# Seven-product second layer in the full chunks of batches 1 to 7 of a fused FFT filter and mixture-of-experts kernel, with the shrink subtractions on GpSimd

## The chip, the core and the metric

The kernel runs on one core of one Trainium2 chip. The time is device time in microseconds (us), median of several executions. Executions of one kernel agree within about 0.3% for the kernel before and within about 1% for the slowest variants here. Engines are named as in the profile: PE is TensorE (PEld its weight loads), DVE is VectorE, ACT is ScalarE, POOL is GpSimd, SP is the engine that issues most DMAs. The kernel's tiles lie in two on-chip memories: the results of matmuls in PSUM, all others in SBUF. An evacuation is a copy of a result out of PSUM.

## The reference, cut to what matters

```python
# x: (8, 2496, 256)
X  = rfft(x, axis=1)                                  # over the 2496 positions
Yr = Xr @ w_r - Xi @ w_i + b_r
Yi = Xr @ w_i + Xi @ w_r + b_i
Y  = sign(Y) * maximum(abs(Y) - 0.01, 0)              # "shrink", on Yr and Yi
x  = irfft(Y, axis=1)
# one expert per batch, chosen from the mean over positions
h      = maximum(x[b] @ w1[e], 0)                     # (2496, 1024)   first layer
out[b] = gate * (h @ w2[e])                           # (2496, 256)    second layer
```

## The kernel before

Each batch passes through a forward transform, a complex product, the shrink, an inverse transform, and then the two expert layers. The batches are pipelined: while batch b is in its expert layers, batch b+1 is in its transforms. A list scheduler inside the program fixes the order of instructions on every engine when the kernel is built, from a planned duration for each operation. On the chip, each engine works through its own list in order: the seven kernels below that share one plan (the changed one, e3 to e7, e9) show the same order of instructions on PE, DVE and ACT, at different times.

**The shrink**, for each of 5 groups of frequency bins in a batch (batches 2 to 7). `z` is the product, `cl` is `z` clamped to plus and minus 0.01, and `Y = z - cl`. Four subtractions move data between the two halves of the partitions:

```python
oc_ = S.op("DVE", 0.34, cl_, vt(f + 0.03), deps=z_ops, lat=0.48)
def y_(_, cell=cell):
    Y = cell["Y"]
    for r in range(2):
        for i in range(2):
            s = slice(64 * i, 64 * i + 64)
            nc.vector.tensor_sub(out=Y[64*r : 64*r+64, :, i],
                                 in0=cell["z"][s, r], in1=cell["cl"][s, r])
oy = S.op("DVE", 1.5, y_, vt(f + 0.03), deps=[oc_], lat=1.62)   # planned: 1.5 us, result after 1.62
```

The inverse transform's matmuls (line L547 in the profile) read `Y`.

**The second layer**, for a chunk of 512 tokens, is by default 32 matmuls of 256 columns (L1438): 4 token tiles times 8 slices of the hidden dimension. In the chunks listed in `FAST` it is done as seven block products in place of eight (Winograd's form of Strassen's product): the chunk's tokens, the hidden dimension and the output columns are each cut in two. That takes 56 matmuls of 128 columns (L1252), four sums of the hidden values on DVE, and combinations of the products on the way out of PSUM:

```python
FAST = {(B - 1, c) for c in range(4)}            # last batch only
# add_fast, per chunk: four DVE sums of 128x1024 fp16, both inputs in SBUF
o1 = S1 = h[0,1] + h[1,1]      # L1219
o2 = S2 = S1 - h[0,0]          # L1222
o3 = S3 = h[0,0] - h[0,1]      # L1226 (in place)
o4 = S4 = h[1,0] - S2          # L1229
# ... seven products; three DVE adds (L1276) and four scaled copies on ACT or DVE (L1267, L1270)
# once per batch, four DVE sums of 128x512 of the second layer's weights: L1193 to L1196
```

## Time and profile before

| | before |
|---|---|
| median of 4 runs | 431.42 us |
| PE busy, of the profiled span | 417.4 us, 97% |
| DVE / ACT / POOL busy | 305.3 / 336.1 / 60.6 us |
| one batch in the repeating middle | 50.0 us |

This is one group of the profile's list; the columns after the bar are busy us, mean ns of one, and the engine's idle time just before these instructions, with what ended it.

```profile
L928 DVE TENSOR_TENSOR tt<-ps,bias 128x512 f16<-128x512 f32 x60 | 38.6, 686 | 18.1 <-PE ps L914 17.9
```

DVE is idle because it waits for PE's results, not the reverse. And this is the same fact for a stretch of exactly two batches (length, then busy us of PE, PEld, DVE, ACT, POOL, each with its count of instructions; then granted PE clock, DMA share, GB/s):

```profile
210.60:310.59 99.99, 99.99 (x839) 75.91 (x838) 78.52 (x163) 78.20 (x154) 15.19 (x26) 1.00 0.86 207
```

PE does not pause at all in these 100 us.

### The profile page before, as it was taken

How to read it: one execution, taken by the hardware profiler on the slowest of the kernel's cores; microseconds unless marked ns; L12 is line 12 of the kernel's file. 1: busy time of each engine (PE TensorE's matmuls, PEld its weight loads, DVE VectorE, ACT ScalarE, POOL GpSimd, SP SyncE). 2: the span in 40 equal slices, each digit the busy share in tenths (PEclk: the TensorE clock that was granted, in tenths of full speed). 3: DMA queues.
4: the chain of work that ended last, by engine and by line, in shares of the span. 5: the costliest groups of instructions: out<-in, count | busy, mean ns of one | idle time of the engine just before them, and what ended most of it. 6: DMA issues, size and time to landing. Idle time of an engine off the chain costs nothing.

```text
span 429.5 us, 9604 instructions
## 1 busy us (share of the span) xinstructions
PE 417.4 (97%) x3601; PEld 315.9 (74%) x3601; DVE 305.3 (71%) x635; ACT 336.1 (78%) x654; POOL 60.6 (14%) x104
## 2 busy tenths in 40 slices
PE   5988999999999999999999999999999999999996
PEld 2557777887777877778677876778777787777775
DVE  1697865777777797787967787677977878414561
ACT  3789888787967887779866798678877788778884
POOL 5553100001003020033000320031200030001000
PEclk9999999999999999999999999999999999999999
DMA  7999797929885996889885998959978276521222
GB/s 151 234 172 163 129 279 238 216 75 181 230 270 106 232 186 195 251 171 203 191 247 194 197 203 209 283 117 218 194 220 253 86 166 126 181 91 56 65 99 92
DMA packets 71847, 76.98 MB, mean 179 GB/s; under 512 B 7128, under 2 KB 45744, under 8 KB 71800
## 3 DMA queue, kind: packets, MB, share of 16 engines
q1 hardware_dynamic: 58834, 56.23, 44.7%
q0 software_dynamic: 12704, 19.88, 29.1%
q8 instruction: 28, 0.46, 0.4%
q10 hardware_dynamic: 262, 0.25, 0.2%
q14 instruction: 19, 0.16, 0.1%
HBM read 57.54 MB, written 37.49 MB: 221 GB/s over the span
## 4 chain that ended last, share of the span: by engine, by line
PE 92%; DVE 3%; DMA 2%; ACT 2%; POOL 1%; issue 1%; SPq 0%; DVEq 0%; POOLq 0%
PE ps L1389 31%; PE ps L1438 27%; PE ps L914 9%; PE ps L718 4%; PE ps L547 4%; PE ps L812 3%; PE ps L1058 3%; PE ps L1252 3%; PE ps L876 3%; PE ps L1323 2%; DMA xin<-in_x_dram 1%; PE ps L751 1%; PE ps L754 1%; DMA ysb<-in_w_i_dram 1%; DVE z L766 1%; ACT ysb L1074 1%
## 5 line engine op out<-in xcount | busy, mean ns | idle before, releaser
L1402 ACT ACTIVATE hs<-ps 128x512 f16<-128x512 f32 (+3 forms) x313 | 172.1, 568 | 65.3 <-PE ps L1389 61.3
L1389 PE MATMUL ps<-ysb,w1s 128*128 128x512 f16 (+3 forms) x688 | 182.6, 359 | 0.1
L1438 PE MATMUL ps<-w2s,hs 128*128 128x256 f16 x1056 | 150.9, 272 | 0.0
L1438 PEld LDWEIGHTS <-hs 128*128 128x128 f16 x1056 | 102.0, 98 | 38.3 <-issue 0.9
L1389 PEld LDWEIGHTS <-w1s 128*128 128x128 f16 x688 | 73.9, 113 | 17.9 <-issue 0.7
L956 DVE TENSOR_TENSOR Y<-z,cl 64x512 f16<-64x512 f16 x120 | 50.4, 420 | 2.7
L928 DVE TENSOR_TENSOR tt<-ps,bias 128x512 f16<-128x512 f32 x60 | 38.6, 686 | 18.1 <-PE ps L914 17.9
L914 PE MATMUL ps<-w,XT 128*128 128x256 f16 x360 | 49.9, 273 | 0.1
L914 PEld LDWEIGHTS <-XT 128*128 128x128 f16 x360 | 34.9, 98 | 9.9 <-DVE XT L895 0.6
L1455 ACT ACTIVATE ost<-ps,gbc 128x512 f32<-128x512 f32 (+1 forms) x57 | 38.4, 675 | 2.7 <-PE ps L1438 1.9
L937 DVE TENSOR_TENSOR z<-ps,tt 128x512 f16<-128x512 f32 x60 | 38.7, 683 | 0.2
L1074 DVE CAST ysb<-ps 128x468 f16<-128x468 f32 (+1 forms) x37 | 21.4, 587 | 22.7 <-PE ps L1058 20.0
L554 ACT CAST V<-ps 128x512 f16<-128x512 f32 x52 | 30.2, 598 | 0.6
L822 ACT CAST A<-ps 120x512 f16<-120x512 f32 x46 | 26.0, 613 | 3.1 <-PE ps L812 3.1
L884 ACT CAST XT<-ps 128x512 f16<-128x512 f32 x41 | 24.3, 596 | 0.0
L1074 ACT CAST ysb<-ps 128x468 f16<-128x468 f32 (+1 forms) x47 | 21.8, 533 | 2.4 <-PE ps L1058 2.4
L1150 POOL DMA_DIRECT2D w1s<-in_moe_w_dram x8 | 6.0, 755 | 122.3 <-PE ps L1058 111.6
L547 PE MATMUL ps<-Y,ti 128*128 128x256 f16 x140 | 23.0, 272 | 0.0
L884 DVE CAST XT<-ps 128x512 f16<-128x512 f32 x19 | 13.1, 689 | 13.8 <-PE ps L876 13.0
L812 PE MATMUL ps<-xin,wa 117*120 117x512 f16 x66 | 22.8, 380 | 0.1
L1404 DVE TENSOR_SCALAR hs<-ps 128x512 f16<-128x512 f32 (+3 forms) x31 | 17.4, 568 | 7.3 <-PE ps L1389 6.5
L1058 PE MATMUL ps<-wi,V 120*128 120x117 f16 (+1 forms) x308 | 22.5, 213 | 0.0
(112 smaller groups left out, 476.5 us busy)
## 6 DMA issues: line engine op xcount, KB each, us to landing
out_dram<-ost SPq DMA_DIRECT2D x71, 256.0 KB
scr<-V SPq DMA_DIRECT2D x35, 256.0 KB
xin<-in_x_dram POOLq DMA_DIRECT2D x21, 390.0 KB, 9.8
XB<-fwd SPq DMA_DIRECT2D x30, 256.0 KB
V<-scr SPq DMA_DIRECT2D x14, 504.0 KB
fwd<-A SPq DMA_DIRECT2D x18, 360.0 KB
w1s<-in_moe_w_dram POOLq DMA_DIRECT2D x8, 512.0 KB, 7.1
w2s<-in_moe_w_dram POOLq DMA_DIRECT2D x8, 512.0 KB, 8.1
```

The lines of the kernel that those rows point to most:

```text
L547: nc.tensor.matmul(pv[:, D * i : D * i + D], ti[:, 4 * q + k, :], cell["Y"](k))
L812: nc.tensor.matmul(pa[0:120, :], wa, xin_t[b][:, xcol(2 * gp) : xcol(2 * gp) + 2 * D])
L884: COPY[eng](out=cell["X"][:, ch, :, 0:2].rearrange("p a r i k -> p a i r k"), in_=hc["p"].rearrange("p (a i r k) -> p a i r k", a=2, i=2, ...
L914: nc.tensor.matmul(pm[:, D * a : D * a + D], cell["X"][:, ch, a, t].rearrange("p i k -> p (i k)"), w4[:, ch, t, :], start=(ch == 0), stop= ...
L928: nc.vector.tensor_add(out=cell["tt"][:, r], in0=cell["T", 2].rearrange("p (a c) -> p a c", a=2), in1=bias[:, r].unsqueeze(1).to_broadcast ...
L937: nc.vector.tensor_add(out=cell["z"][:, r], in0=cell["T", 1 - r].rearrange("p (a c) -> p a c", a=2), in1=cell["tt"][:, r])
L956: nc.vector.tensor_sub(out=Y[64 * r : 64 * r + 64, :, i], in0=cell["z"][s, r], in1=cell["cl"][s, r])
L1074: COPY[eng](out=yv[:, :, 12 * gb : 12 * gb + 3 * nf].rearrange("p a (g j) -> p a g j", j=3), in_=pi[:, 0 : 117 * nf].rearrange("p (g a j) ...
L1389: nc.tensor.matmul(ph[:, 0:nl], w1v[:, ch, fc // 4, :, fc % 4], ysb_t[b][:, ch, ns : ns + nl], start=(ch == 0), stop=(ch == 1))
L1402: nc.scalar.activation(out=o, in_=i, func=AFT.Relu)
L1438: nc.tensor.matmul(oc["p"][:, i, :], cell["hs"][:, ft, ts], w2s_t[b][:, ft, :], start=(ft == 0), stop=(ft == E - 1))
L1455: nc.scalar.activation(out=ost[:, 0:n], in_=oc["p"][:, 0:n], func=AFT.Copy, scale=gbc_t[b])
```

## The change

The intent is to save PE columns: the seven-product form is to serve all full chunks of batches 1 to 7. DVE gets much work by that, so the shrink subtractions go to GpSimd, which is nearly idle. The token tiles of the seven-product form take alternate tokens, so that a partition holds two neighbouring rows of the output and stores them as one run.

```diff
-    FAST = {(B - 1, c) for c in range(4)}
+    FAST = {(b, c) for b in range(1, B) for c in range(4)}
@@ shrink
-                        nc.vector.tensor_sub(
+                        nc.gpsimd.tensor_sub(
                             out=Y[64 * r : 64 * r + 64, :, i],
                             in0=cell["z"][s, r], in1=cell["cl"][s, r])
-            oy = S.op("DVE", 1.5, y_, vt(f + 0.03), deps=[oc_], lat=1.62)
+            oy = S.op("POOL", 4.9, y_, vt(f + 0.03), deps=[oc_], lat=5.1)
@@ add_fast: token tiles (one of the seven operands shown)
-        A = {"11": lambda f, t: cell["hs"][:, f, m * t : m * t + m],
+        A = {"11": lambda f, t: cell["hs"][:, f, t:th:2],
...
-                        "(i p) c -> p i c", p=m),
+                        "(p i) c -> p i c", i=2),
```

The scheduler is thus told that the four GpSimd subtractions take 4.9 us, with the result after 5.1.

More of the change, by code (lines that the diff above doesn't have):

```diff
@@ L1234, in add_fast @@
         o4 = s_op("s4", 0, s4, vt(0.3), [o2])
-        A = {"11": lambda f, t: cell["hs"][:, f, m * t : m * t + m],
-             "12": lambda f, t: cell["hs"][:, 4 + f, m * t : m * t + m],
-             "22": lambda f, t: cell["hs"][:, 4 + f, th + m * t : th + m * t + m],
-             "S3": lambda f, t: cell["hs"][:, f, th + m * t : th + m * t + m],
-             "S1": lambda f, t: fc["S"][:, 0, f, m * t : m * t + m],
-             "S2": lambda f, t: fc["S"][:, 1, f, m * t : m * t + m],
-             "S4": lambda f, t: fc["S"][:, 2, f, m * t : m * t + m]}
+        A = {"11": lambda f, t: cell["hs"][:, f, t:th:2],
+             "12": lambda f, t: cell["hs"][:, 4 + f, t:th:2],
+             "22": lambda f, t: cell["hs"][:, 4 + f, th + t : nl : 2],
+             "S3": lambda f, t: cell["hs"][:, f, th + t : nl : 2],
+             "S1": lambda f, t: fc["S"][:, 0, f, t:th:2],
+             "S2": lambda f, t: fc["S"][:, 1, f, t:th:2],
+             "S4": lambda f, t: fc["S"][:, 2, f, t:th:2]}
         w2 = lambda k, h: lambda f: w2s_t[b][:, 4 * k + f, P * h : P * h + P]
```

## The prediction

> **What bounds the kernel now.** I read the page's engine row first, then the table of equal windows over the repeating middle, then the groups of instructions, then the chain that ended last.
>
> ```profile
> PE 417.4 (97%) x3601; PEld 315.9 (74%) x3601; DVE 305.3 (71%) x635; ACT 336.1 (78%) x654; POOL 60.6 (14%) x104
> ...
> 200.00:250.00 50.00, 50.00 (x421) 37.85 (x419) 39.26 (x81) 39.02 (x77) 7.59 (x13) 1.00 0.85 204
> 250.00:300.00 50.00, 50.00 (x423) 38.05 (x421) 39.26 (x81) 39.19 (x77) 7.61 (x13) 1.00 0.87 206
> ...
> PE 92%; DVE 3%; DMA 2%; ACT 2%; POOL 1%; issue 1%; SPq 0%; DVEq 0%; POOLq 0%
> ```
>
> The window rows give length, then busy time of PE, PEld, DVE, ACT and POOL. One batch takes about 50 us (its first L812 matmuls stand in the chain at 210.60, 260.68 and 310.59), and in such a window PE is busy all of it at full clock, DVE 39.3, ACT 39.2, POOL 7.6. Busy PE need not be PE at its peak, so I checked the pace: in the chain 8 matmuls of 256 columns take 0.87 us, 8 of 128 columns 0.45, 24 of them 1.34. That is 109 and 56 ns each, within a few ns of columns over 2.4 GHz. So **TensorE's column stream is the bound**; DVE and ACT have 10.7 us of idle time each per batch.
>
> **What the Trainium skill says.** (1) "TensorE: Matmul & The Clock Gate", Back-to-back issue gap: an isolated gap is N/2.4 + 2.5 ns, but a sustained stream with weight loads is given as about 81 ns at N=128. The trace disagrees with the 81: 56 ns with a load each. I use 56. (2) "SBUF — State Buffer", Who interferes with whom: a DVE instruction with two SBUF inputs, or in a two-port mode, shares a port with a GpSimd instruction that reads SBUF, and the second to issue blocks until the first has finished. The kernel before has one spot that agrees:
>
> ```profile
> 19.91 1.50 POOL L420 TENSOR_SCALAR V<-tf 128x512 f16<-128x512 f16 x1
> 21.37 0.78 POOL L422 COPY V<-tf 128x512 f16<-128x512 f16 x1
> ...
> 20.84 0.16 DVE L1122 TENSOR_SCALAR lsb<-ps 128x8 f32<-128x8 f32 x1
> 20.96 0.73 DVE L779 TENSOR_SCALAR cl<-z 128x1024 f16<-128x1024 f16 x1
> 21.73 0.97 DVE L781 TENSOR_TENSOR Y<-z,cl 128x1024 f16<-128x1024 f16 x1
> ```
>
> The columns are start and duration. The DVE clamp, normally 0.43 us, takes 0.73 when it starts 0.45 before the end of a GpSimd instruction; the subtraction of two SBUF tiles, normally 0.69, takes 0.97 when it starts 0.42 before the end of the next. Each loses what remained of the GpSimd instruction, less some 0.15 us[...]. DVE instructions that read PSUM keep their 0.68 there. (3) "GPSIMD Engine Reference", Performance versus the Vector engine: about 2.6 cycles per element for two inputs. At its 1.2 GHz, 512 elements make 1.11 us plus dispatch; I estimate 1.2 us for one 64x512 subtraction. The trace before has none.
>
> **The change part by part.** The durations that I use:
>
> ```profile
> L956 DVE TENSOR_TENSOR Y<-z,cl 64x512 f16<-64x512 f16 x120 | 50.4, 420 | 2.7
> L1276 DVE SCALAR_TENSOR_TENSOR ost<-ps,gbc,ost 128x256 f32<-128x256 f32 x12 | 5.8, 482 | 10.5 <-ACT ost L1267 7.7 <-PE ps L1252 2.8
> L1226 DVE TENSOR_TENSOR hs<-hs 128x1024 f16<-128x1024 f16 x4 | 2.7, 684 | 0.0
> ```
>
> *TensorE.* 24 more chunks (4 in each of batches 1 to 6) take the seven-product form. Each drops 32 matmuls of 256 columns and adds 56 of 128: 32 x 109 = 3.48 us out, 56 x 56 = 3.11 in, so -0.36 us a chunk, -1.45 a batch, **-8.7 us in all**. That is 2.0% and the most the change can give, at a period of 48.5 us.
>
> *Alternate-token tiles.* Weight loads now step by two elements. L1438 already does that and takes 98 ns a load, as the contiguous loads of L1252 do; only the step of four of L1389 takes 113. Nothing lost on PE. Output rows stay in runs of two tokens, so the stores keep their shape. Worth zero by itself.
>
> *DVE.* I took the changed instruction counts from the compiled order and the durations from the groups above. Over the kernel: +96 sums of 128x1024 at 0.687 = +65.9; +24 weight sums at 0.42 = +10.1; +76 combining instructions at 0.482 = +36.6; -120 subtractions = -50.4; evacuations moved to ACT and back by the kernel's own scheduler, net -15. Sum +47 us over 6 batches, or +7.8 of summed duration; neighbours overlap by some 5%, so I take **39.3 + 7.3 = 46.6 us busy per batch**. That is already 96% of the 48.5 that PE would need.
>
> *ACT.* +92 evacuations of 128x256 at 0.483 = +44.4, -47 output evacuations = -32, +22 ysb casts = +12.4, rest nearly even: +25 us, about 43.5 per batch. Busy, but not the bound.
>
> *GpSimd.* 20 subtractions per batch, 20 x 1.2 = 24 us on top of 7.6: 32 us of 50. Not the bound, but its chain clamp, subtract, inverse matmul grows from 1.7 to about 5 us for each of 5 groups, which the static order allows for.
>
> *Port.* Here lies the decision. DVE instructions of a batch that use two SBUF inputs or the two-port mode: 16 sums, 4 weight sums, 5 XT sums, 5 clamps, 30 in all. Each clamp releases four GpSimd subtractions, 4.8 us in a row, and the compiled DVE order often puts sums right behind a clamp. I walked one batch by hand, letting DVE run back to back and the two engines take turns. Behind clamp 1 stand four weight sums: three wait for a whole subtraction, about 1.1 us each, 3.4 in all. Clamp 2: two isolated sums, 0.45 + 0.95 = 1.4. Clamp 3: one, 1.05. Clamp 4: three, 3.1. Clamp 5: three, 2.95. **Sum 11.9 us a batch if the port is locked as the two events above suggest.** Then DVE needs 46.6 + 11.9 = 58.5 us, a period 8.5 over today's, and six periods make +51: about 482 us. If the port is only shared, or the waits partly fall into DVE's idle time, I put 4 to 6 us a batch: a period of 51 to 53, so 438 to 450.
>
> **The rivals.**
> 1. *TensorE stays the bound.* The port costs little, 46.6 us of DVE hides under 48.5, and the time is 431.6 - 8.7 = 423 plus a few us of stalls: 424 to 430. For it: DVE idles waiting for PE today (17.9 us before L928, 20.0 before L1074), and that slack can be eaten first. Against: 96% on an in-order engine leaves PSUM banks waiting, and the two collisions above were not free.
> 2. *DVE becomes the bound through the port*: 438 to 482, as worked out. For it: the two stretched instructions, and 24 us of reads placed in front of DVE's sums. Against: only two events, both against one-input GpSimd instructions.
> 3. *The longer subtraction chain stalls TensorE.* If four subtractions take 7 us instead of the 5 that the order was made for, the inverse matmuls (L547) wait up to 2 us five times a batch, up to +10 us a batch at worst, mostly the same time as in 2. Deferred x and weight loads behind subtractions in the GpSimd queue belong here too. The x loads have a slack of many us: the queue stood 31 us before the copy that heads them.
> 4. *Transfers.* Bytes do not change; DMA share of 0.85 stays. I give this nothing.
>
> **Range and chances.** Faster by over 2% needs 423.1 or less, which is the whole of the 8.7 us with no stall anywhere: 4%. Within 2% (up to 440) needs a period under 51.4, port waits plus stalls under some 4.8 us a batch: 26%. Slower: 70%. I weigh rival 1 by a fifth to a quarter, sharing or partial hiding by a quarter, the full lock by half, but trim the hand walk, since DVE falling behind spreads the collisions out: about 6 us a batch over the PE floor. 423 + 6 x 5 = **453 us**, range 427 to 482.
>
> **What would show each step.** PE: 1568 matmuls in L1252 at a pace of 56 ns where eight run together, and 288 left in L1438; if the pace is slower, the stride costs and the first step is wrong. DVE: windows of one batch with DVE busy near its whole length and PE well below it; if DVE shows 46 to 47 and PE all, rival 1 holds. Port: the mean of the sums (L1219, L1222, L1226, L1229) above 0.9 us instead of 0.687, L1193 to L1196 far above 0.42, while L928 and L937, which read PSUM, keep 0.68; if all keep their durations, the lock was wrong. GpSimd: L956 near 1.2 us when undisturbed. Chain: L547 idling for the GpSimd Y would show rival 3; the chain that ended last should move from 92% PE to a mix with DVE and POOL.
> The prediction is wrong most likely if GpSimd's subtraction is much shorter than 1.2 us or does not hold the port.

## The result and the profile after

The changed kernel takes **474.54 us** (4 runs, 472.51 to 476.92) against 431.42: 1.10 times as long, interval 1.094 to 1.106. Ratios here are the mean of one kernel's fast runs over that of the other's of the same rounds, so not quite the ratio of the medians. The predicted 453 us was too low by 21.5, in the right direction and inside the range (427 to 482).

The page of the changed kernel, its engine row, its chain that ended last, and the group of the moved subtractions:

```profile
PE 425.8 (90%) x4177; PEld 320.6 (67%) x4177; DVE 382.8 (81%) x686; ACT 353.8 (74%) x723; POOL 215.5 (45%) x224
...
PE 63%; DVE 24%; issue 6%; POOL 3%; ACT 1%; DMA 1%; DVEq 0%; ACTq 0%; POOLq 0%
...
L956 POOL TENSOR_TENSOR Y<-z,cl 64x512 f16<-64x512 f16 x120 | 153.9, 1282 | 160.6 <-DVE cl L946 97.5
```

PE fell from 97% to 90% of the span, and its share of the chain from 92% to 63%. DVE came into the chain. Two batches of the repeating middle, in the columns of the window row above:

```profile
221.91:338.29 116.38, 102.88 (x1032) 77.91 (x1030) 103.89 (x177) 85.18 (x178) 67.44 (x66) 0.97 0.74 176
```

The window runs, as the one before the change, from one batch's first L812 matmuls in the chain to those of two batches later. A batch takes 116.38 / 2 = **58.2 us** where it took 50.0. DVE is busy 51.9 us of it. Which waits does PE now have? This is the list of waits of PE in the changed kernel (who waited for whom; total us, times, longest):

```profile
PE ps L1058 <- DVE ysb L1074: 12.9, 5, 2.6
PE ps L914 <- DVE XT L895: 11.8, 13, 1.8
PE ps L1389 <- DVE hs L1404: 4.1, 2, 2.1
...
PE ps L1252 <- DVE ost L1270: 3.1, 2, 1.6
PE ps L812 <- DVE A L822: 2.5, 1, 2.5
PE ps L1252 <- DVE S L1222: 1.8, 6, 0.8
...
PE ps L547 <- POOL Y L956: 0.4, 2, 0.2
```

The six DVE lines add to 36.2 us, near the 37 us by which PE's idle time grew (475.2 - 425.8 = 49.4 against 429.5 - 417.4 = 12.1). PE waits for DVE, in many places, and hardly ever for the GpSimd result itself (0.4 us). Now DVE. Groups by shape, sums first, then an instruction that reads PSUM:

```profile
L1226 DVE TENSOR_TENSOR hs<-hs 128x1024 f16<-128x1024 f16 x28 | 29.6, 1058 | 0.0
L1222 DVE TENSOR_TENSOR S<-S,hs 128x1024 f16<-128x1024 f16 x28 | 29.6, 1057 | 0.6
L1219 DVE TENSOR_TENSOR S<-hs 128x1024 f16<-128x1024 f16 x28 | 25.3, 905 | 0.1
L1195 DVE TENSOR_TENSOR T<-w2s 128x512 f16<-128x512 f16 x7 | 7.7, 1100 | 0.0
...
L928 DVE TENSOR_TENSOR tt<-ps,bias 128x512 f16<-128x512 f32 x60 | 39.0, 680 | 1.8 <-PE ps L914 1.7
```

The sums that took 0.68 us in batch 7 of the kernel before now take about 1.0 on average, three of the four weight sums 1.0 to 1.1 for 0.42 (the first, L1193, kept its 0.42), while the addition from PSUM kept its 0.68. The clamp, with one input, kept its 0.42 as a rule, but took 1.38 in 2 of 30 cases. One spot shows why. The time line of DVE, then that of POOL, over the same microseconds (start, duration):

```profile
302.98 0.68 DVE L1219 TENSOR_TENSOR S<-hs 128x1024 f16<-128x1024 f16 x1
303.70 1.53 DVE L1222 TENSOR_TENSOR S<-S,hs 128x1024 f16<-128x1024 f16 x1
305.15 1.64 DVE L1226 TENSOR_TENSOR hs<-hs 128x1024 f16<-128x1024 f16 x1
306.71 0.68 DVE L1229 TENSOR_TENSOR S<-hs,S 128x1024 f16<-128x1024 f16 x1
```

```profile
301.81 1.16 POOL L956 TENSOR_TENSOR Y<-z,cl 64x512 f16<-64x512 f16 x1
303.02 1.66 POOL L956 TENSOR_TENSOR Y<-z,cl 64x512 f16<-64x512 f16 x1
304.75 1.48 POOL L956 TENSOR_TENSOR Y<-z,cl 64x512 f16<-64x512 f16 x1
```

The two engines take turns. A sum starts at 302.98; the GpSimd subtraction of 303.02 then needs 1.66 in place of 1.15: it waited about half a microsecond for that sum, and ended at 304.68. The next sum, issued at 303.70, ends at 305.23, which is 0.55 after that subtraction ended. The last subtraction ends at 306.23, and the sum issued at 305.15 ends at 306.79. With the series over, the fourth sum takes 0.68 again.

The trace also ties these sums to PE's waits. Between 110 and 410 us PE waited 20 times for over 0.8 us, and at each of them DVE was at a sum stretched to 1.2 us or more, or had been less than 1.5 us earlier. The five waits at L1058, up to 2.6 us and 12.9 in all, stand behind stretched weight sums (L1194 to L1196).

### The profile page after: what moved, and what is told of

Its sections match the earlier page's. It is cut to its first block, busy times and chain, and to the rows that moved or that the text cites. A ratio compares the mean times of both kernels' runs of the same rounds, so it can differ in the third digit from the quotient of the medians.

```text
span 475.2 us, 11058 instructions
## 1 busy us (share of the span) xinstructions
PE 425.8 (90%) x4177; PEld 320.6 (67%) x4177; DVE 382.8 (81%) x686; ACT 353.8 (74%) x723; POOL 215.5 (45%) x224
## 4 chain that ended last, share of the span: by engine, by line
PE 63%; DVE 24%; issue 6%; POOL 3%; ACT 1%; DMA 1%; DVEq 0%; ACTq 0%; POOLq 0%
PE ps L1389 21%; PE ps L1252 13%; PE ps L914 7%; PE ps L1438 5%; PE ps L718 3%; DVE S L1222 3%; PE ps L812 2%; PE ps L1323 2%; DVE S L1219 2%; PE ps L547 2%; POOL Y L956 2%; PE ps L876 2%; DVE S L1229 2%; DVE z L937 2%; PE ps L1058 2%
## 5 line engine op out<-in xcount | busy, mean ns | idle before, releaser
L956 POOL TENSOR_TENSOR Y<-z,cl 64x512 f16<-64x512 f16 x120 | 153.9, 1282 | 160.6 <-DVE cl L946 97.5
L1267 ACT ACTIVATE ost<-ps,gbc 128x256 f32<-128x256 f32 x108 | 51.9, 481 | 24.0 <-PE ps L1252 23.4
L1276 DVE SCALAR_TENSOR_TENSOR ost<-ps,gbc,ost 128x256 f32<-128x256 f32 x84 | 40.2, 479 | 30.7 <-ACT ost L1267 18.2
L1252 PEld LDWEIGHTS <-S 128*128 128x128 f16 x672 | 43.6, 98 | 15.9 <-DVE S L1222 4.4
L1074 ACT CAST ysb<-ps 128x468 f16<-128x468 f32 x68 | 32.8, 545 | 18.4 <-PE ps L1058 18.4
L1438 PE MATMUL ps<-w2s,hs 128*128 128x256 f16 x288 | 40.8, 272 | 0.0
L1252 PE MATMUL ps<-T,hs 128*128 128x128 f16 x448 | 35.2, 223 | 3.2 <-DVE ost L1270 3.1
L1252 PE MATMUL ps<-T,S 128*128 128x128 f16 x448 | 34.1, 219 | 2.2 <-DVE S L1222 1.8
L1404 DVE TENSOR_SCALAR hs<-ps 128x512 f16<-128x512 f32 (+3 forms) x44 | 26.6, 609 | 10.2 <-PE ps L1389 9.7
L1058 PE MATMUL ps<-wi,V 120*128 120x117 f16 (+1 forms) x308 | 23.0, 216 | 13.0 <-DVE ysb L1074 12.9
L1252 PE MATMUL ps<-w2s,hs 128*128 128x128 f16 x448 | 34.0, 219 | 0.0
L1058 PEld LDWEIGHTS <-V 120*128 120x128 f16 x308 | 19.9, 99 | 15.3 <-issue 13.6
```

The lines of the kernel that those rows point to most:

```text
L956: nc.gpsimd.tensor_sub(out=Y[64 * r : 64 * r + 64, :, i], in0=cell["z"][s, r], in1=cell["cl"][s, r])
L1058: nc.tensor.matmul(pi[:, 117 * i : 117 * i + M], V2[:, g, ch * P : ch * P + P], w)
L1074: COPY[eng](out=yv[:, :, 12 * gb : 12 * gb + 3 * nf].rearrange("p a (g j) -> p a g j", j=3), in_=pi[:, 0 : 117 * nf].rearrange("p (g a j) ...
L1252: nc.tensor.matmul(fc[dst[0]][0:m, dst[1], t, :], A[a](f, t), bb(f), start=start and t == 0 and f == 0, stop=f == 3, skip_group_check=True)
L1267: nc.scalar.activation(out=ost(t, h), in_=src, func=AFT.Copy, scale=gbc_t[b][0:m])
L1276: nc.vector.scalar_tensor_tensor(out=ost(t, h), in0=fc["F"][0:m, half], scalar=gbc_t[b][0:m], in1=ost(t, h), op0=ALU.mult, op1=ALU.add)
```

## The experiments

Theories. **Port:** GpSimd subtractions and DVE instructions with two SBUF inputs block each other; the sums stretch, DVE falls behind, and PE waits for DVE. **Load:** DVE has too much work, collisions or not. **Chain:** the path clamp, subtraction, inverse matmul became too long for the fixed order, and PE waits for GpSimd. **Tiles:** the alternate tokens cost PE or DMA something. Twelve kernels were run, in three lots; times of the kernel before in the same lots were 431.64, 431.68 and 431.12 us. e5 and e6 were executed twice, the others four to six times.

| run | differs from | time, us | ratio to before (95%) |
|---|---|---|---|
| e1_no_gpsimd | after: subtractions on DVE | 438.17 | 1.016 (1.014 to 1.017) |
| e2_gpsimd_only | before: subtractions on GpSimd | 432.72 | 1.004 (1.001 to 1.006) |
| e3_write_only | after: GpSimd writes 8 constants | 426.94 | 0.990 (0.988 to 0.992) |
| e4_contig_tiles | after: contiguous tiles | 475.84 | 1.103 (1.101 to 1.105) |
| e5_write_only_long | after: GpSimd writes 12 constants | 474.10 | 1.098 (1.094 to 1.103) |
| e6_read_copy | after: GpSimd copies, one input | 464.28 | 1.075 (1.073 to 1.078) |
| e7_split_subs | after: subtractions halved | 458.59 | 1.062 (1.060 to 1.064) |
| e8_two_chunks | e1: two of four chunks | 434.13 | 1.005 (1.004 to 1.007) |
| e9_write_only_ten | after: GpSimd writes 10 constants | 442.69 | 1.027 (1.026 to 1.029) |
| e10_longer_in_order | after: scheduler told 6.6 us | 478.27 | 1.110 (1.106 to 1.113) |
| e11_half_dose | after: two of four chunks | 444.26 | 1.030 (1.028 to 1.032) |
| e12_write_only_in_order | e10: GpSimd writes 12 constants | 447.37 | 1.037 (1.035 to 1.038) |

### The parts of the change, one at a time

**e1: subtractions back on DVE.**

```diff
-                        nc.gpsimd.tensor_sub(
+                        nc.vector.tensor_sub(
-            oy = S.op("POOL", 4.9, y_, vt(f + 0.03), deps=[oc_], lat=5.1)
+            oy = S.op("DVE", 1.5, y_, vt(f + 0.03), deps=[oc_], lat=1.62)
```

> The changed kernel with the shrink subtractions back on DVE; seven-product form and alternate-token tiles stay. Port theory (GpSimd subtractions and DVE sums block each other): the four kinds of sums go back to 0.68 us each, but DVE gets 8.4 us a batch of subtractions back, 46.6 + 8.4 = 55 us busy per batch, so DVE stays the bound: 458 to 470 us. Load theory (DVE simply has too much work, the port adds nothing): this must be slower than the changed kernel, over 480. Chain theory (the long wait for the GpSimd result stalls TensorE, DVE has room): back to 424 to 432.

Measured 438.17, a miss for all: much better than the port theory's number, against the load theory, and not quite the chain theory's. A hundred microseconds of its middle, and one kind of sum:

```profile
210.00:310.00 100.00, 98.11 (x1018) 74.78 (x1016) 96.12 (x207) 83.80 (x181) 15.14 (x26) 1.00 0.83 201
```

```profile
L1226 DVE TENSOR_TENSOR hs<-hs 128x1024 f16<-128x1024 f16 x28 | 19.1, 683 | 0.0
```

The sums are back at 0.68. DVE is busy 96% of the time, and yet PE gets 98%. My 55 us of DVE per batch was too much for two reasons: the kernel's scheduler hands more evacuations to ACT (740 ACT instructions for the changed kernel's 723), and neighbouring DVE instructions overlap by more than I had allowed. What follows: DVE carrying all the work, subtractions included, is 36 us faster than DVE relieved of them. The load theory falls.

**e2: the GpSimd subtractions alone, in the kernel before.** The same two lines of diff as in e1, the other way, applied to the kernel before.

> The kernel before with only the shrink subtractions moved to GpSimd. Port theory: DVE falls to about 31 us a batch, only the 5 clamps and 5 XT sums of a batch can collide and few do; TensorE stays the bound: 430 to 437. Load theory: the same, 430 to 433. Chain theory: five stalls of 1 to 2 us a batch, 455 to 470.

Measured 432.72, as port and load said. GpSimd was nearly as busy as in the changed kernel (199.9 us for 215.5), but there are few DVE instructions with two SBUF inputs to collide with. Those that there are do stretch: the XT sums (L895) took 0.607 us on average for 0.42, and the four weight sums of batch 7 took 1.26 to 1.38. DVE had room for it.

So each half alone costs little, 6.5 us and 1.1 us, and both together 43. The other 35 us exist only where DVE's sums and GpSimd's subtractions are in the kernel at once.

**e4: contiguous tiles in the changed kernel.**

```diff
-        A = {"11": lambda f, t: cell["hs"][:, f, t:th:2],
+        A = {"11": lambda f, t: cell["hs"][:, f, m * t : m * t + m],   # and so for all seven
-                        "(p i) c -> p i c", i=2),
+                        "(i p) c -> p i c", p=m),
```

> The changed kernel with the contiguous token tiles of the kernel before in the seven-product form (output rows stored one token at a time). All theories that put the cost on DVE and GpSimd: 470 to 478, as the changed kernel. If the weight loads with a step of two cost TensorE time: faster by 1% or more; if one-token rows load the DMA queues: slower by 1% or more.

Measured 475.84, the changed kernel's time within its scatter. The tiles are not where the time went, in either direction.

### Is it the reading of SBUF?

**e3: GpSimd as busy, but only writing.** One subtraction of two columns makes GpSimd wait for the clamp; then eight constant writes into `Y`. Its output is wrong, which doesn't matter for the time. The scheduled order is that of the changed kernel.

```diff
                 Y = cell["Y"]
+                nc.gpsimd.tensor_sub(out=Y[:, 0, 0, 0:2], in0=cell["z"][:, 0, 0, 0:2],
+                                     in1=cell["cl"][:, 0, 0, 0:2])
                 for r in range(2):
                     for i in range(2):
-                        s = slice(64 * i, 64 * i + 64)
-                        nc.gpsimd.tensor_sub(out=Y[64*r : 64*r+64, :, i],
-                                             in0=cell["z"][s, r], in1=cell["cl"][s, r])
+                        for _h in range(2):
+                            nc.gpsimd.memset(Y[64*r : 64*r+64, :, i], 0.01)
```

> The changed kernel, where GpSimd reads two elements of z and cl in one small subtraction and then writes a constant into Y eight times, about as long as the four subtractions, but reading no SBUF (wrong result on purpose). Port theory with blocking by GpSimd reads only: sums back to 0.68 us, 46.6 us of DVE a batch fits, 425 to 437 us. Load theory and chain theory: sums keep what they have or the waits stay, 465 to 480.

Measured **426.94 us**, 1.0% below the kernel before. The lines of this file are shifted by two, so L1228 is the in-place sum, L1226 in the others:

```profile
L1228 DVE TENSOR_TENSOR hs<-hs 128x1024 f16<-128x1024 f16 x28 | 19.1, 683 | 0.0
```

With the same DVE list and the same PE list, and GpSimd nearly as busy (193.1 us), the sums are undisturbed and the change would be a small gain. But one point was not clean: eight writes with their small subtraction last 4.6 us (median), while the four real subtractions last 4.8 to 5.9 in the changed kernel (median 5.3). A chain that is shorter than real might hide a chain effect. So I made it longer.

**e5: twelve writes**, `range(3)` in place of `range(2)` above.

> As the write-only stand-in, with twelve constant writes instead of eight: 12 x 0.52 + 0.3 = 6.6 us from the clamp to the end of Y, longer than the four real subtractions under collision (5.1 to 5.6 us). Port theory: GpSimd still reads nothing, the sums stay at 0.68 us, 425 to 434 us. Chain theory (the length of the GpSimd step stalls TensorE): at or above the changed kernel, 465 to 490.

Measured 474.10 us: the changed kernel's own time, against my expectation. Had I looked at the time alone, the port theory would have fallen here. The same sum, and the longest wait of PE:

```profile
L1228 DVE TENSOR_TENSOR hs<-hs 128x1024 f16<-128x1024 f16 x28 | 19.1, 684 | 0.0
```

```profile
PE ps L547 <- POOL Y L959: 39.6, 36, 1.4
```

The sums are undisturbed; PE loses 39.6 us waiting for GpSimd at the inverse matmuls, a wait that came to 0.4 us in the changed kernel. The same 474 us, by another way. The chain theory names a real effect, and a strong one, since PE has no slack: the series took 6.9 us where 4.9 were planned, and PE lost 1.1 us on average at each of 36 waits. But it is not the effect that the changed kernel's trace shows.

**e9: ten writes** (three in place of two at two of the four places), meant to last 5.5 us. The trace has 5.7 to 6.2, median 5.8, so longer than the real series' median of 5.3.

> The write-only stand-in with ten constant writes: 0.3 + 10 x 0.52 = 5.5 us from clamp to Y, as long as the four real subtractions of the changed kernel last under collision (5.1 to 5.6 us), sums undisturbed. Eight writes (4.6 us) gave 426.9, twelve (6.6 us) 474.1, with TensorE waiting about 1.1 us at 36 inverse matmuls. Port theory: only the part of the chain over the 5.1 us that the static order plans for stalls TensorE, 0.3 to 0.5 us at some 30 groups: 434 to 444, so at least 30 of the changed kernel's 43 us belong to the port. Chain theory (the changed kernel's loss is the length of its GpSimd step): 465 to 475.

Measured 442.69, within the port theory's 434 to 444. Of the 47.6 us between e3 and the changed kernel, a chain of that length makes at most 15.8 (442.7 - 426.9), and the remaining 31.9 need the reading (some 7 of them by way of the PE clock; see "Left open"). Undisturbed, the series would not be 5.3 us long either: in e2 the median subtraction took 1.152 us, and four with their gaps 4.8. The excess length is a product of the collisions too.

### Does the plan's ignorance explain it?

**e10 and e12: the same plan, reading and not reading.** Both tell the scheduler 6.6 us, so that it puts the inverse matmuls later. e10 keeps the real subtractions; e12 has the twelve writes, which really take that long (6.9 us in the trace).

```diff
-            oy = S.op("POOL", 4.9, y_, vt(f + 0.03), deps=[oc_], lat=5.1)
+            oy = S.op("POOL", 6.6, y_, vt(f + 0.03), deps=[oc_], lat=6.8)
```

> The changed kernel with its scheduler told that the GpSimd step takes 6.6 us (6.8 to the result) instead of 4.9 (5.1): the static order puts the inverse matmuls later; no other change. Port theory: the sums keep their means near 1 us and DVE stays late, 455 to 475 us. Chain theory: the stalls vanish, 424 to 435.

> As the run before the last (scheduler told 6.6 and 6.8 us), with the twelve constant writes (6.6 us) in place of the subtractions; same scheduled order, GpSimd reads almost nothing. Port theory: the 474 us of twelve writes under the old order was the order's ignorance of the length, so now 425 to 436, and the gap to the run that reads is the port's. If a long chain stalls TensorE whatever the order: 455 to 475.

(The "run before the last" of the second text is e10.) Measured 478.27 and 447.37. A plan that knows the length does not help the real change at all, so the chain theory falls for it. With the same planned operations and costs, and a GpSimd series that is even longer, not reading is 30.9 us faster. That is near the 31.9 above, from another pair; the two kernels have the same order of instructions on PE, DVE and ACT, and the same clock (0.98). But e12 missed the port theory's 425 to 436. The plan did remove the waits at L547 (1.0 us left of 39.6), and others came. The first line is PE's longest wait in e12 (first-layer matmuls for DVE's evacuations), the second DVE's wait in front of a transpose of the output:

```profile
PE ps L1391 <- DVE hs L1406: 15.6, 4, 4.0
DVE ost L1350 <- DMA out_dram<-ost: 19.9, 4, 5.0
```

At each of PE's four waits DVE stood idle for 4.9 to 5.0 us, and the trace puts that down to an output transfer; I take it that the transpose waited for an output buffer to come free. No sum was stretched (longest 0.69). PE was also busy 418.6 us for e3's 410.6, at a lower clock. These 15.6 and 8.0 us are about the 23.2 between the two profiled spans, so e12's excess over e3 is not one of collisions; a later `Y` is not free even when it is planned.

### How long does one collision last?

**e7: each subtraction cut in two; e6: eight copies of one input each.** If a DVE sum waits for the rest of one GpSimd instruction, the longest sum must follow the length of that instruction.

```diff
# e7, right result
-                        nc.gpsimd.tensor_sub(out=Y[64*r : 64*r+64, :, i],
-                                             in0=cell["z"][s, r], in1=cell["cl"][s, r])
+                        for a in range(2):
+                            nc.gpsimd.tensor_sub(out=Y[64*r : 64*r+64, a, i],
+                                                 in0=cell["z"][s, r, a], in1=cell["cl"][s, r, a])
# e6, as e3 with copies (z is not shrunk; the comparison's tolerance lets it pass)
-                            nc.gpsimd.memset(Y[64*r : 64*r+64, :, i], 0.01)
+                            nc.gpsimd.tensor_copy(out=Y[64*r : 64*r+64, :, i], in_=cell["z"][s, r])
```

> The changed kernel with each of the four GpSimd subtractions cut into two of half the columns (eight of about 0.65 us; right result). If the engines take turns instruction by instruction, the longest sum falls from 1.64 to about 1.2 us, but more sums find a subtraction to wait for: 450 to 470 us. If the port is held for the whole series of subtractions, or the waiting depends on GpSimd's total time alone: 472 to 482.

> As the write-only stand-in, with eight copies of z into Y, each reading one SBUF operand and lasting about 0.5 us (wrong result on purpose, nothing is shrunk). If a GpSimd read blocks a DVE sum for the rest of that one instruction: sums of up to 0.68 + 0.5 = 1.2 us, means near 0.85, 438 to 462 us. If only two-input GpSimd instructions block: sums 0.68 and 425 to 434. If the length of the single GpSimd instruction does not matter, only its total: 465 to 478.

Measured 458.59 and 464.28; e7 as expected, e6 just above its range. Minimum, median and maximum ns of one kind of sum and of the GpSimd instructions, first in e7, then in e6 (whose lines are shifted by four):

```profile
L1227 DVE TENSOR_TENSOR hs<-hs x28: 677/1152/1159, 112.4 to 445.0; 128x1024 f16<-128x1024 f16 x28
...
L957 POOL TENSOR_TENSOR Y<-z,cl x240: 657/670/1237, 81.7 to 401.6; 64x256 f16<-64x256 f16 x120
```

```profile
L1230 DVE TENSOR_TENSOR hs<-hs x28: 679/886/1096, 112.7 to 450.4; 128x1024 f16<-128x1024 f16 x28
...
L960 POOL COPY Y<-z x240: 602/612/1162, 82.2 to 404.6; 64x512 f16<-64x512 f16 x120
```

| GpSimd instruction | undisturbed (shortest), us | longest in-place sum, us | over 0.68 |
|---|---|---|---|
| write, one constant (e3) | 0.52 (mean) | 0.68 | 0 |
| copy, 64x512 (e6) | 0.60 | 1.10 | 0.42 |
| half subtraction, 64x256 (e7) | 0.66 | 1.16 | 0.48 |
| subtraction, 64x512 (after) | 1.14 | 1.64 | 0.96 |

The longest delay is the GpSimd instruction's length less 0.18 us in all three cases that read, and nothing where it only writes. In these cases one input or two does not matter, the length does. Seen from the other side, the GpSimd instruction's own maximum is 0.5 to 0.6 us over its minimum, about the length of one sum. The times of e6 and e7 are not the price of reading alone: their series lasted 6.6 and 6.5 us (median), and PE lost 26.6 us in e6 waiting for them at L547. e7 is 16 us faster than the changed kernel with the same arithmetic, though its series of eight is longer: its longest PE wait for anything in the middle is 1.9 us, but it does lose 15.8 us at L547, where the chain now shows. (Its clock was 1.00, so part of the 16 may be the clock's.)

### Looking for a version that beats both

**e8: two of four chunks, no GpSimd. e11: two of four chunks, with GpSimd (scheduler told 5.6 and 5.8 us).** e8 starts from e1, e11 from the changed kernel:

```diff
-    FAST = {(b, c) for b in range(1, B) for c in range(4)}
+    FAST = {(b, c) for b in range(1, B) for c in range(4)
+            if b == B - 1 or c % 2 == 0}
```

> The seven-product form in two of the four full chunks of batches 1 to 6 (all four in batch 7), subtractions on DVE, alternate-token tiles. TensorE saves 2 x 0.36 us a batch, 4.3 us in all; DVE needs 39.3 + 2 x 4 + 1.7 = 49 us at the old split, some of which the kernel's scheduler hands to ACT, so about 45. If TensorE stays the bound: 427 to 430, 0.5 to 1% under the kernel before. If DVE near its limit takes it back, as it does with four chunks: 430 to 436.

> GpSimd subtractions with the scheduler told 5.6 us (5.8), and the seven-product form in two of four full chunks of batches 1 to 6. DVE needs 31 + 8 + 1.7 = 41 us a batch undisturbed and has room for 3 to 5 us of blocking; TensorE saves 4.3 us. Port theory: sums still stretched, to means of 0.9 us or so, but mostly in DVE's idle time: 429 to 442. If the loss follows the number of sums in proportion, half of 43 us: 450 to 456. It beats both kernels if TensorE's saving comes through: 427 to 430.

Measured 434.13 and 444.26. e8 lies in the second of its two ranges: between the kernel before and e1 (438.17), so with the subtractions on DVE two chunks cost 2.5 us and four 6.5; neither pays. One and three were not run. e11 missed its range by 2 us. In it DVE is busy only 83% of the time (124.87 us of 150 in its middle), so it is not out of throughput, and still PE waits for DVE's evacuations:

```profile
PE ps L1390 <- DVE hs L1405: 10.4, 6, 2.7
```

At the five longest of these six waits the trace has two or three sums of 1.5 to 1.65 us in a row in DVE's list. A stretched sum is late at once for what stands behind it in DVE's list, whether or not DVE has room on average. No correct version that I ran beats the kernel before; e3 shows that some 5 us would be there for one whose GpSimd part reads nothing, which these subtractions cannot do.

## Why the prediction was right, and where its terms were off

**The bound and the saving.** Right. Eight matmuls of 128 columns still stand in the chain of the changed kernel at 0.45 us, and e3, where nothing stretches, gains 4.7 us of the 8.7 that I called the most to be had.

**Alternate tiles: nothing.** Right (e4).

**DVE's work of 46.6 us a batch.** Too high. In e3 DVE is busy 86.7 us in the 98.76 of two batches, so 43.3 a batch. I allowed 5% for the overlap of neighbours; back to back, instructions of 0.68 us follow each other every 0.60, which is 12%. My claim that 96% of an in-order engine leaves banks waiting was also too dark: e1 runs DVE at 96% for 1.6% of time.

**Port waits of 11.9 us a batch, by hand.** The mechanism was right, the size too high. In the two batches above, the 32 sums took 33.6 us for 22.0, the eight weight sums 8.7 for 3.4, and the ten XT sums 4.9 for 4.2: 17.6 in all, 8.8 a batch.

**The sum of the two, a period of 58.5 us.** It was met within 0.3 us (58.2), but not as I built it. I had 46.6 + 11.9 with DVE never idle. Measured were 43.2 + 8.8 + 6.2, the last being DVE's idle time, when it waits for ACT and PE, which wait for DVE. Two terms were too high and one was missing; they cancelled. So the agreement is luck, and no support for the single terms.

**The 453 us.** I took 482 from the full walk and then trimmed it, "since DVE falling behind spreads the collisions out". That is the step that failed: falling behind did not spread them. A clamp frees four subtractions, and the sums that stand behind it in DVE's fixed list meet them anew in every changed batch, 8.8 us of them in a batch. The last sum does not follow from its own words either: "about 6 us a batch" over the walk's six batches makes 423 + 36 = 459, not 453. What the walk itself had too much, from 482 to 474.5, lies at both ends: from the second layer's last matmuls (L1323) of one batch to those of the next, batches 2 to 5 took 7.5 to 9.4 us longer than before the change, the last changed batch 4.2, and batch 1 ended only 6.5 later.

**The rivals.** Rival 1 (PE stays the bound, 424 to 430) is what e3 shows without the reads. Rival 3, the chain, was said to cost mostly the same time as rival 2. It is a separate effect, and e5 shows that it could have made the same total alone; in the changed kernel it is held down to 0.4 us of waiting, because PE is already late by DVE.

**Left open: the clock.** In the changed kernel, e4, e10 and e12 the mean granted PE clock was 0.98, in the kernel before, e1 and e7 it was 1.00. The mean hides that the clock went to half for short times. This is one of them in the changed kernel, in the columns of the window rows (the clock is the third number from the end):

```profile
329.72:333.10 3.38, 3.38 (x29) 3.24 (x28) 0.99 (x3) 1.56 (x4) 0.61 (x1) 0.50 0.84 134
```

Its trace has six such stretches of 3.41 us, each beginning within 1.5 us of the end of a PE wait of 1.8 to 2.6 us; two other waits of 2.5 us or more were followed by none. e12 has four, each with one of its four waits of 3.8 to 4.0 us; e1 and e7, with no wait over 1.9 in the middle, have none there; e5, with waits of at most 1.4, has one. So the low clock mostly goes with long waits, but I did not test the waits as its cause. Over the four executions of the changed kernel the time falls from 476.9 us at a clock of 0.978 to 472.5 at 0.988; continued to full clock that makes about 467, an estimate from these four. So some 7 of the 43 us go with the clock. They are in the 31.9 us between e9 (clock 1.00) and the changed kernel, but not in the 30.9 between e12 and e10.

## What to carry to other kernels

Before giving work to an idle GpSimd, list which VectorE instructions have two SBUF inputs and stand near it in time: here each one that met a reading GpSimd instruction was delayed by what remained of it, less about 0.2 us, and on a full pipeline this cost 43 us with VectorE busy 81% and GpSimd 45% of the time. Where an engine such as PE has no slack, read its waits and not only the total: e5 and the changed kernel both took 474 us, one waiting for GpSimd, the other for DVE. If such work must go to GpSimd, short instructions delayed less than long ones here, and those that only write did not delay the two-input instructions at all (longest sum 0.69 us). They are not free for all: in e3, e5, e9 and e12 a few clamps, with one input, took 0.5 to 0.85 us for 0.42 when they met constant writes.

## What the Trainium skill lacked or had wrong

- "SBUF — State Buffer", Who interferes with whom, was right that a GpSimd instruction which reads blocks a DVE instruction with two SBUF inputs and that one which only writes does not. It has no measured delay for this pair. The runs show a longest delay of the GpSimd instruction's length less 0.18 us (0.60 gave 0.42, 0.66 gave 0.48, 1.14 gave 0.96), for a GpSimd copy with one input as for subtractions with two.
- "GPSIMD Engine Reference", Performance versus the Vector engine: its 2.6 cycles per element for two inputs, with dispatch estimated at 0.1 us, made 1.2 us; 64x512 fp16 took 1.15. It lacks numbers for fp16 tiles of this size: 0.66 us for 64x256, 0.60 for a copy of 64x512, 0.52 for a constant write of 64x512.
- "TensorE: Matmul & The Clock Gate", Back-to-back issue gap, gives about 81 ns for a sustained stream of N=128 with weight loads. Here 8 such matmuls, each with its load, took 0.45 us, 56 ns each.
- No page that I read says what a delayed instruction does to an in-order engine on a full pipeline: 8.8 us of stretched DVE instructions a batch made the batch 8.2 us longer, although DVE had 6.2 us of idle time left.
